# One-hots laid out by columns, past counts added in PSUM by VectorE, and a preparation handed to the first block's products: a convolution, router and mixture-of-experts kernel

## The chip, the cores and the metric

The kernel runs on one core of a Trainium2 chip. The metric is the device time of one execution in microseconds. The engines are called as in the profile: PE (TensorE, matrix products; PEld its weight loads), DVE (VectorE), ACT (ScalarE), POOL (GpSimd) and SP (SyncE, which issues most of the DMAs). SBUF is the working memory, PSUM the memory into which PE writes.

## The reference

```python
def _attn_ref(x, weight):                      # x [8, 3584, 192], weight [8 heads, 7 taps]
    w = softmax of weight over the taps
    x_pad = np.concatenate([zeros of 6 rows, x], axis=1)
    ...
    out = np.einsum('hk,bskhg->bshg', w, x_unf)   # each head's 24 columns: causal filter of 7 taps

def _moe_ref(x, w_skip, w_gate, w1, w2):       # x [28672, 192], 8 experts, w1 [8, 192, 1024], w2 [8, 1024, 192]
    do_compute = x @ w_skip > 0
    out = x.copy()
    xc = x[do_compute]
    logits = xc @ w_gate
    e_idx = np.argmax(logits, axis=1)
    ...                                        # probs: softmax of the logits
    gate_w = probs[np.arange(len(xc)), e_idx]
    for e in range(E):
        mask = e_idx == e
        h = np.maximum(xc[mask] @ w1[e], 0.0)
        y[mask] = gate_w[mask, None] * (h @ w2[e])
    out[do_compute] = xc + y
    return out
```

Tokens go through a causal filter; those with a positive skip score then go through the expert with the highest logit, weighted by its probability. All is fp32.

## The kernel before

**Phase 1** goes over the 8 batches. A batch of 3584 tokens is 30 columns (`NC`) of 120 tokens (`R`), with the token on the partition. `conv_heads` makes the filter as products with banded matrices, and ACT copies the results to `ys`, from where SP stores them to the output. Behind the heads of a batch, in small steps written out by hand (`IR`, `RR`, `PICK`), run the routing of the batch before (`route`: `router`, then `slots`) and the inversion of an earlier one (`invert`). The routines are generators: each `yield` hands over to the next, and the order in which the instructions are emitted is the order in which each engine runs them (`manual_schedule`).

**`slots`** finds each token's place in its expert's list. From the logits `lg` (9 for each token: 8 experts and the skip score) DVE makes the maximum (L546), the differences `df` (L550), the keys `kq` (L555), their minimum `km` (L560, L562) and from these the one-hots `oh`, fp16, 8 experts for each of 240 = 30 x 8 pairs (L566). PE then makes two products with `oh`: with a matrix of ones, for the count of each expert in each column (L571), and with a triangular matrix, for each token's rank in its column (L573). Between them a third product, fp32 with one row, adds `hist[b]`, the counts of all past batches, to the first column of each expert (L572). All three write the PSUM tile `pr`. DVE sums the counts over the columns with a scan (L583), adds the ranks (L589), copies the last column to `hist[b + 1]` (L591), takes the entry of the token's own expert by a product with `oh` (L598) and a sum (L601), and the slots are split for the inversion (L604 to L633).

**`invert`** turns slots into lists of token numbers: DVE makes one-hots `oa` and `ob` of the slot's row and column (L658), PE multiplies them and accumulates in `inv` (L646).

**The blocks.** 256 tokens of one expert make a block (128 for some). The first eight blocks (`TAIL`, `NTAIL`) come from the lists of the first five batches and are worked on while the last batches are routed. `gather` fetches the rows `y` (POOL, L829), `prep` scales and splits them to fp16 (DVE L845 to L362, ACT L853 and L854, DVE L859) and transposes them into `m` by DMA (SP, L862). `up` and `down` are the two products (L888, L939) with the Relu and the split of its result between them (ACT L909, DVE L911); `finish_rows` adds the result to the rows (L925), and POOL scatters it (L927). `weave` runs such a product's generator and at each of its steps a step of the routing and inversion that is left (`tail_slot`), and `n` pieces of the preparations in the list that it is given.

During the last batch's heads `step7` gathers four blocks and gives out pieces of the preparations of the first `PREP0` = 3 blocks, `PSEQ[h]` at head h. A call of `prep_piece` runs one `next` of the current preparation; one that has ended is dropped, and the call goes on with the next block.

```python
PSEQ = (0, 0, 4, 3, 4, 3, 4, 3)
TAIL = ("2221", "2221")
PREP0 = 3
```

The weights of the experts are split to two fp16 parts in the background (`split_weights`, ACT L327, DVE L338); what is left of it after the last head is emitted at once (`background(-1)`).

Of the kernel before, what the change touches and what calls it, by code (L numbers as in the profile page):

```python
# [8 lines left out]
F16 = mybir.dt.float16  # L9
I32 = mybir.dt.int32  # L10
AF = mybir.ActivationFunctionType
ALU = mybir.AluOpType
# [8 lines left out]
E, F = 8, 1024  # L21
NTOK = B * S
NF = F // P
R = 120
# [3 lines left out]
NC = -(-S // R)  # L28
# [43 lines left out]
FIRSTP = ((), ("", "y4"), ("", "y5"))  # L72
# [19 lines left out]
AHEAD = 5  # L92
PREP = 3
PREP0 = 3
MBUF = 4
PU = 2
# [6 lines left out]
def conv_router_moe(ctx: ExitStack, tc: tile.TileContext, x, weight, w_skip, w_gate, w1, w2, out):  # L103
    nc = tc.nc
# [11 lines left out]
    wk1 = ph1.enter_context(tc.tile_pool(name="wk1", bufs=2, side="right"))  # L116
# [47 lines left out]
    ones32 = const.tile([1, P], F32, name="ones32")  # L164
# [10 lines left out]
    ones16 = const.tile([P, P], F16, name="ones16")  # L175
# [77 lines left out]
    um1 = const.tile([P, P], F16, name="um1")  # L253
# [112 lines left out]
    hist = const.tile([P, B + 1, E], F32, name="hist")  # L366
# [168 lines left out]
    def slots(b, lg):  # L535
        def t3(name):
            return wk1.tile([R, NC, E], F32, tag=name, bufs=1, name=f"{name}{b}")

        def t2(name, dt=F32, bufs=1):
            return wk1.tile([R, NC], dt, tag=name, bufs=bufs, name=f"{name}{b}")  # L540

        def bc(t):
            return t.unsqueeze(2).broadcast_to([R, NC, E])
# [10 lines left out]
        kq = t3("kq")  # L554
        nc.vector.scalar_tensor_tensor(out=kq, in0=df, scalar=0.0,  # L555
                                       in1=pri[0:R].unsqueeze(1).broadcast_to([R, NC, E]),
                                       op0=ALU.is_equal, op1=ALU.mult)
        yield
        km = t2("km")
# [2 lines left out]
        nc.vector.scalar_tensor_tensor(out=km, in0=lg[:, 0:NC, E], scalar=0.0, in1=km,  # L562
                                       op0=ALU.is_le, op1=ALU.add)
        yield
        oh = wk1.tile([R, E, NC], F16, tag="oh", name=f"oh{b}")
        nc.vector.tensor_tensor(out=oh.rearrange("p e c -> p c e"), in0=kq, in1=bc(km), op=ALU.is_equal)  # L566
        yield HOP
        if in_tail:
            yield HOP
        pr = ps_ms.tile([P, 2, E, NC], F32, tag="ms", name=f"pr{b}")  # L570
        nc.tensor.matmul(pr[:, 0], ones16[0:R, :], oh, start=True, stop=False)  # L571
        nc.tensor.matmul(pr[:, 0, :, 0], ones32, hist[0:1, b, :], start=False, stop=True)  # L572
        nc.tensor.matmul(pr[0:R, 1], um1[0:R, 0:R], oh, start=True, stop=True)  # L573
        sm = t2("sm")
        nc.vector.tensor_reduce(out=sm, in_=ex, axis=AX.X, op=ALU.add)
        yield
# [2 lines left out]
        gt = gate_all[0:R, b, :]  # L579
        nc.vector.reciprocal(out=gt, in_=sm)  # L580
        yield HOP
        run = wk1.tile([P, E, NC], F32, tag="df", bufs=1, name=f"run{b}")
        nc.vector.tensor_tensor_scan(out=run.rearrange("p e c -> p (e c)"),  # L583
                                     data0=smask.rearrange("p e c -> p (e c)"),
# [3 lines left out]
        rs = wk1.tile([R, E, NC], F32, tag="kq", bufs=1, name=f"rs{b}")  # L588
# [4 lines left out]
        if b == REL:  # L593
# [1 line left out]
            yield  # L595
            nc.vector.scalar_tensor_tensor(out=hist[:, b + 1, 0:NA], in0=eoff[:, 0:NA], scalar=float(KH * P),
                                           in1=hist[:, b + 1, 0:NA], op0=ALU.add, op1=ALU.max)
        nc.vector.tensor_tensor(out=rs, in0=rs, in1=oh, op=ALU.mult)  # L598
        yield HOP
        sl = t2("sl")  # L600
        nc.vector.tensor_reduce(out=sl, in_=rs.rearrange("p e c -> p c e"), axis=AX.X, op=ALU.add)  # L601
# [11 lines left out]
                                op=ALU.is_ge)  # L613
# [177 lines left out]
    def early(what, after):  # L791

        if what:
            nc.gpsimd.tensor_copy(pace, after)
            gather(blocks[int(what[1])])

    preps, begun = [], [0]

    def prep_piece():
        if not preps:  # L800
            if begun[0] == PREP0:
                return
            preps.append(prep(blocks[begun[0]]))
            begun[0] += 1
        if next(preps[0], preps) is preps:
            preps.pop(0)
            prep_piece()
# [33 lines left out]
    def prep(k):  # L841

        am = k.am = wk2.tile([P, 2], F32, tag="yam", bufs=6, name=f"yam{k.n}")
        sc = wk2.tile([P, 2], F32, tag="ysc", bufs=3, name=f"ysc{k.n}")
        nc.vector.tensor_reduce(out=am[:, 0:k.us], in_=k.y[:, 0:k.us], axis=AX.X, op=ALU.max, apply_absolute_value=True)  # L845
        yield
        yield from pow2_steps(am[:, 0:k.us], sc[:, 0:k.us])
        yield


        yt = wk2.tile([P, 2, 4 * P], F16, tag="yt", bufs=3, name=f"yt{k.n}")
        for u in range(k.us):
            nc.scalar.activation(yt[:, u, 0:D], k.y[:, u, :], AF.Copy, scale=sc[:, u:u + 1])  # L853
            nc.scalar.activation(yt[:, u, 3 * P:], k.y[:, u, D - P:D], AF.Copy, scale=sc[:, u:u + 1])  # L854
        yield
        k.m = wk2.tile([P, 4, BLK], F16, tag="m", bufs=MBUF, name=f"m{k.n}")
        for u in range(k.us):
            for (a, b_, o) in ((P, D, D), (0, P, D + 64)):
                nc.vector.scalar_tensor_tensor(out=yt[:, u, o:o + b_ - a], in0=k.y[:, u, a:b_],  # L859
                                               scalar=sc[:, u:u + 1], in1=yt[:, u, a:b_],  # L860
                                               op0=ALU.mult, op1=ALU.subtract)
            nc.sync.dma_start_transpose(out=k.m[:, :, u * P:(u + 1) * P], in_=yt[:, u, :])  # L862
            yield
# [7 lines left out]
    def bank(pools):  # L871
        pools.append(pools.pop(0))
        return pools[-1]

    def up(k, wt):
        k.hh = wk3.tile([P, NF, BLK], F16, tag="hh", bufs=2, name=f"hh{k.n}")
        k.hl = wk3.tile([P, NF, BLK], F16, tag="hl", bufs=2, name=f"hl{k.n}")
        w = k.us * P
        fs = 2 * BLK // w
        split = len(ph_pools) > 1  # L880
        banks = []

        def open_bank(f0):
            banks.append(bank(ph_pools).tile([P, 2 * BLK], F32, tag="ph", name=f"ph{k.n}_{f0}")
                         .rearrange("p (f w) -> p f w", w=w))

        def product(ph, f, o, m, q, start, stop):
            nc.tensor.matmul(ph[:, f % fs, :], wt[q, o + f * P:o + (f + 1) * P], k.m[q, m, 0:w], start=start, stop=stop,  # L888
                             skip_group_check=split)

        if split:


            for f0 in range(0, NF, fs):
                open_bank(f0)
            for i in range(0, len(banks), 2):
                for j in range(fs):
                    for h in range(2):
                        product(banks[i + h], (i + h) * fs + j, OW1L + F, 1 + 2 * h, slice(64 * h, 64 * h + 64), j == 0, False)
        for f0 in range(0, NF, fs):  # L900
            if not split:
                open_bank(f0)
            ph = banks[f0 // fs]
            for f in range(f0, f0 + fs):
                seq = ((OW1, 0), (OW1, 2), (OW1 + F, 1), (OW1L, 0)) + (() if split else ((OW1L + F, 1),))
                for n, (o, m) in enumerate(seq):
                    product(ph, f, o, m, slice(0, P), n == 0 and not split, n == len(seq) - 1)
            hh = k.hh[:, f0:f0 + fs, 0:w]
            nc.scalar.activation(hh, ph, AF.Relu)  # L909
            yield  # L910
            nc.vector.scalar_tensor_tensor(out=k.hl[:, f0:f0 + fs, 0:w], in0=ph, scalar=0.0, in1=hh,  # L911
                                           op0=ALU.max, op1=ALU.subtract)
# [39 lines left out]
    blocks = []  # L952
# [42 lines left out]
    def weights_of(n):  # L995
        k = blocks[n]
        return wts[k.e] if k.l is None else dynw[k.l]
# [170 lines left out]
    def tail_slot():  # L1168

        background()  # L1170
        if not listed:
            turns((routes, 0), (routes, 1), (inversions, 0))
            if not routes and not inversions:
                finish(final_lists())
                listed.append(True)
        elif tables:
            if next(tables[0], tables) is tables:
                tables.pop()

    def weave(gen, preps=(), n=0, first=()):  # L1180

        k, *first = first or (None,)
        for f, _ in enumerate(gen):
            if first and f % 2 == 0:
                early(first.pop(0), k.hh[0:1, f * 2 * BLK // (k.us * P), 0:1])
            tail_slot()
            for _ in range(n):
                for p in list(preps):
                    if next(p, p) is p:
                        preps.remove(p)  # L1190
                    else:
                        break

    routes.append(whole_route(B - 1))
    in_tail.append(1)
    gathered, prepped = AHEAD - 1, PREP0
    ahead = []
    while preps or begun[0] < PREP0:
        prep_piece()
    bg.extend(save_weights(e, wts[e]) for e in range(NA))  # L1200
    weave(up(blocks[0], weights_of(0)), first=(blocks[0], *FIRSTP[0]))
    for n in range(NBLK):
        k = blocks[n]
        if 0 < n < 5:
# [30 lines left out]
        if n < 2:  # L1235
            gathered = AHEAD + n
# [15 lines left out]
    with tc.If(left > 0):  # L1252
# [9 lines left out]
        for c in range(B * NC):  # L1262
            nc.gpsimd.indirect_dma_start(
                out=list_dr, out_offset=bass.IndirectOffsetOnAxis(ap=slot[0:R, c:c + 1], axis=0),
                in_=ids[0:R, c:c + 1], in_offset=None, bounds_check=E * SPAN - 1, oob_is_err=False)
        for e in range(E):
            first = nc.values_load(lo_hi[0:1, e:e + 1], min_val=0, max_val=NTOK // BLK)
            last = nc.values_load(lo_hi[0:1, E + e:E + e + 1], min_val=0, max_val=NTOK // BLK)
            with tc.For_i(first, last, 1) as i:
# [4 lines left out]
                    out=k.si, in_=list_dr[bass.ds(i * BLK + e * SPAN, BLK), :].rearrange("(u p) o -> p (u o)", p=P))  # L1274
# [35 lines left out]
```

## Time and profile before

| | us |
|---|---|
| median of three runs | 684.56 (684.56 to 689.15) |
| the profiled execution | 686.43 |
| its span, first to last instruction | 684.7 |
| busy in the span: PE, DVE, ACT, POOL | 656.2, 544.3, 352.1, 271.0 |
| L566, one-hots, eight times | 9.7 |
| L571 + L572 + L573, products, matmuls alone | 2.1 + 3.3 + 2.6 |
| L598, product with the one-hots, eight times | 4.7 |

The profile is of one execution. A row of a group names line, engine, operation, output and inputs, their shapes and the count; behind the bar stand the busy time of the group, the mean of one in ns, and how long the engine idled just before, with what released it. A row with "min/median/max" is of the view of one line. Busy times of PE overlap, since its matmuls are pipelined; what one costs is better read from the distance between starts.

### The profile page before, as it was taken

To read this page: it belongs to the slowest core of one execution; us is meant where nothing else is said; L and a number is where in the kernel's file an instruction comes from. 1 tells how busy PE (TensorE), PEld (TensorE's weight loads), DVE (VectorE), ACT (ScalarE), POOL (GpSimd) and SP (SyncE) were. 2 spreads that over 40 slices of the span, in tenths; PEclk is the share of its full clock that TensorE was granted. 3 is DMA by queue.
4 is the path that set the end of the run, shared out by engine and by line. 5 is a ranking of instruction groups with operands and counts; after the bars stand their busy time and mean duration, and the time that the engine had idled before them with its cause. 6 is when DMAs were issued, how large, how long until landed. Compare 5 with 4: busy or idle time off the path is not lost.

```text
span 684.7 us, 17904 instructions
## 1 busy us (share of the span) xinstructions
PE 656.2 (96%) x6586; PEld 563.9 (82%) x6586; DVE 544.3 (79%) x1617; ACT 352.1 (51%) x762; POOL 271.0 (40%) x301
## 2 busy tenths in 40 slices
PE   8999998999697999989999999999999999999995
PEld 7667676766587898979999899999999899999995
DVE  8159999988989989886997897888888876666652
ACT  4776585558742334554464464564554644444421
POOL 4111111124113454644554554644544555554322
PEclk9999999999999999999999999999999999999999
DMA  7999999962941657466359369578567456999970
GB/s 214 322 322 313 300 286 326 326 217 66 246 145 47 161 143 153 89 181 182 82 170 216 89 175 193 105 175 177 126 181 157 132 148 175 272 291 330 326 211 15
DMA packets 169127, 133.31 MB, mean 195 GB/s; under 512 B 74320, under 2 KB 155986, under 8 KB 169028
## 3 DMA queue, kind: packets, MB, share of 16 engines
q1 hardware_dynamic: 157988, 110.26, 60.1%
q0 software_dynamic: 11040, 21.80, 11.8%
q8 instruction: 54, 0.88, 0.5%
q14 instruction: 45, 0.37, 0.2%
HBM read 69.70 MB, written 48.04 MB: 172 GB/s over the span
## 4 chain that ended last, share of the span: by engine, by line
PE 55%; DVE 0%; POOL 0%; POOLq 0%; issue 0%
PE ph L888 28%; PE po L939 27%; POOL out_dram L927 0%; DVE hl L911 0%; POOLq L1251 0%; DVE yt L859 0%; DVE o L925 0%
## 5 line engine op out<-in xcount | busy, mean ns | idle before, releaser
L909 ACT ACTIVATE hh<-ph 128x512 f16<-128x512 f32 x230 | 136.2, 593 | 227.1 <-PE ph L888 226.1
L888 PE MATMUL ph<-m,wt 128*128 128x256 f16 (+2 forms) x2000 | 210.0, 270 | 4.4 <-DVE hl L911 2.8
L888 PEld LDWEIGHTS <-wt 128*128 128x128 f16 (+1 forms) x2000 | 167.5, 98 | 38.7 <-issue 17.9
L939 PE MATMUL po<-wt,hh 128*128 128x192 f16 x1536 | 194.2, 246 | 0.0
L911 DVE SCALAR_TENSOR_TENSOR hl<-ph,hh 128x512 f16<-128x512 f32 x230 | 157.5, 686 | 40.9 <-ACT hh L909 40.5
L939 PE MATMUL po<-wt,hl 128*128 128x192 f16 x768 | 188.9, 246 | 0.0
L939 PEld LDWEIGHTS <-hh 128*128 128x128 f16 x1840 | 166.5, 98 | 1.1
L927 POOL DMA_INDIRECT out_dram<-o,sidx x82 | 85.8, 1046 | 138.7 <-DVE o L925 119.4
L829 POOL DMA_INDIRECT y<-out_dram,sidx x82 | 85.3, 1041 | 26.8 <-issue 10.1
L939 PEld LDWEIGHTS <-hl 128*128 128x128 f16 x920 | 90.0, 98 | 0.0
L393 PE MATMUL pc<-xs,toep 128*120 128x384 f32 (+1 forms) x224 | 77.3, 467 | 0.0
L925 DVE SCALAR_TENSOR_TENSOR o<-po,yf,y 128x192 f32<-128x192 f32 x115 | 47.2, 417 | 37.0 <-PE po L939 30.8
L859 DVE SCALAR_TENSOR_TENSOR yt<-y,ysc,yt 128x64 f16<-128x64 f32 x230 | 62.2, 313 | 14.8 <-ACT yt L853 13.2
L395 ACT COPY ys<-pc 120x768 f32<-120x768 f32 (+1 forms) x56 | 42.6, 761 | 40.7 <-PE pc L393 31.8
L853 ACT ACTIVATE yt<-y,ysc 128x192 f16<-128x192 f32 x115 | 51.4, 447 | 19.4 <-DVE ysc L362 13.8
L393 PEld LDWEIGHTS pc<-xs,toep 128*120 128x120 f32 x224 | 36.5, 183 | 14.1 <-issue 0.4
L854 ACT ACTIVATE yt<-y,ysc 128x128 f16<-128x128 f32 x115 | 44.8, 389 | 0.0
L338 DVE SCALAR_TENSOR_TENSOR wt<-raw,ar,wt 128x512 f16<-128x512 f32 x56 | 42.2, 759 | 1.4 <-ACT wt L327 1.4
L327 ACT ACTIVATE wt<-raw,ar 128x512 f16<-128x512 f32 x56 | 38.9, 724 | 5.3 <-DVE ar L362 5.3
L888 PE MATMUL ph<-m,wd 128*128 128x256 f16 (+3 forms) x440 | 40.6, 258 | 0.0
L939 PE MATMUL po<-wd,hh 128*128 128x192 f16 x304 | 38.4, 246 | 0.0
L888 PEld LDWEIGHTS <-wd 128*128 128x128 f16 (+1 forms) x440 | 32.9, 97 | 6.6 <-issue 3.4
(213 smaller groups left out, 778.8 us busy)
## 6 DMA issues: line engine op xcount, KB each, us to landing
wd<-wscr SPq DMA_DIRECT2D x44, 449.0 KB
wscr<-wt SPq DMA_DIRECT2D x84, 128.0 KB
xs<-in_x_dram SPq DMA_DIRECT2D x7, 1440.0 KB
xs<-in_x_dram SPq DMA_DIRECT2D x7, 1248.0 KB
out_dram<-ys SPq DMA_DIRECT2D x6, 1344.0 KB
out_dram<-ys SPq DMA_DIRECT2D x6, 1092.0 KB
raw<-in_moe_w_dram SPq DMA_DIRECT2D x32, 192.0 KB
raw<-in_moe_w_dram SPq DMA_DIRECT2D x8, 512.0 KB
```

The lines of the kernel that those rows point to most:

```text
L393: nc.tensor.matmul(pc[0:R, i, 0:n * G], toep[:, h + i, :], xs[b, half][:, :, (h + i) * G:(h + i + 1) * G], start=True, stop=True)
L395: nc.scalar.copy(ys[b, half][0:R, :, h * G:(h + 2) * G].rearrange("p g (h c) -> p h g c", c=G), pc[0:R, :, 0:n * G].rearrange("p i (g c) - ...
L829: rows_apart(nc.gpsimd.indirect_dma_start(out=k.y[:, u, :], out_offset=None, in_=out[0:k.rows, :], in_offset=bass.IndirectOffsetOnAxis(ap= ...
L853: nc.scalar.activation(yt[:, u, 0:D], k.y[:, u, :], AF.Copy, scale=sc[:, u:u + 1])
L854: nc.scalar.activation(yt[:, u, 3 * P:], k.y[:, u, D - P:D], AF.Copy, scale=sc[:, u:u + 1])
L859: nc.vector.scalar_tensor_tensor(out=yt[:, u, o:o + b_ - a], in0=k.y[:, u, a:b_], scalar=sc[:, u:u + 1], in1=yt[:, u, a:b_], op0=ALU.mult, ...
L888: nc.tensor.matmul(ph[:, f % fs, :], wt[q, o + f * P:o + (f + 1) * P], k.m[q, m, 0:w], start=start, stop=stop, skip_group_check=split)
L909: nc.scalar.activation(hh, ph, AF.Relu)
L911: nc.vector.scalar_tensor_tensor(out=k.hl[:, f0:f0 + fs, 0:w], in0=ph, scalar=0.0, in1=hh, op0=ALU.max, op1=ALU.subtract)
L925: nc.vector.scalar_tensor_tensor(out=o[:, u, :], in0=part, scalar=f2[:, u:u + 1], in1=k.y[:, u, :], op0=ALU.mult, op1=ALU.add)
L927: rows_apart(nc.gpsimd.indirect_dma_start(out=out[0:k.rows, :], out_offset=bass.IndirectOffsetOnAxis(ap=k.si[:, u:u + 1], axis=0), in_=o[: ...
L939: nc.tensor.matmul(part, lhs[:, f, u * P:(u + 1) * P], wt[:, w + f * D:w + (f + 1) * D], start=(n == 0), stop=(n == 3 * NF - 1))
```

## The change

Four edits. The one-hots are laid out with the expert innermost, so that L566 writes them in order; PE reads them in order as before and writes `pr`, whose layout stays, with a stride of one expert's 30 columns; L598 reads them with a stride of 8. The product with `hist` goes, and DVE adds `hist[:, b, :]` to the first column of each expert in PSUM, ahead of the scan. The loop that runs the remaining pieces of the preparations ahead of the first block's up products goes; the preparation at hand is given to the first block's `weave`, two pieces (`PU`) at a step; `prepped`, the number of preparations begun, is taken from the counter.

```diff
-        oh = wk1.tile([R, E, NC], F16, tag="oh", name=f"oh{b}")
-        nc.vector.tensor_tensor(out=oh.rearrange("p e c -> p c e"), in0=kq, in1=bc(km), op=ALU.is_equal)
+        oh = wk1.tile([R, NC, E], F16, tag="oh", name=f"oh{b}")
+        nc.vector.tensor_tensor(out=oh, in0=kq, in1=bc(km), op=ALU.is_equal)
...
-        nc.tensor.matmul(pr[:, 0], ones16[0:R, :], oh, start=True, stop=False)
-        nc.tensor.matmul(pr[:, 0, :, 0], ones32, hist[0:1, b, :], start=False, stop=True)
-        nc.tensor.matmul(pr[0:R, 1], um1[0:R, 0:R], oh, start=True, stop=True)
+        nc.tensor.matmul(pr[:, 0].rearrange("p e c -> p c e"), ones16[0:R, :], oh, start=True, stop=True)
+        nc.tensor.matmul(pr[0:R, 1].rearrange("p e c -> p c e"), um1[0:R, 0:R], oh, start=True, stop=True)
...
+        nc.vector.tensor_tensor(out=pr[:, 0, :, 0], in0=pr[:, 0, :, 0], in1=hist[:, b, :], op=ALU.add)
         run = wk1.tile([P, E, NC], F32, tag="df", bufs=1, name=f"run{b}")
...
-        nc.vector.tensor_tensor(out=rs, in0=rs, in1=oh, op=ALU.mult)
+        nc.vector.tensor_tensor(out=rs, in0=rs, in1=oh.rearrange("p c e -> p e c"), op=ALU.mult)
...
-    gathered, prepped = AHEAD - 1, PREP0
-    ahead = []
-    while preps or begun[0] < PREP0:
-        prep_piece()
+    gathered, prepped = AHEAD - 1, begun[0]
+    ahead = list(preps)
     bg.extend(save_weights(e, wts[e]) for e in range(NA))
-    weave(up(blocks[0], weights_of(0)), first=(blocks[0], *FIRSTP[0]))
+    weave(up(blocks[0], weights_of(0)), ahead, PU, first=(blocks[0], *FIRSTP[0]))
```

## The prediction

> **What bounds the kernel now.** I read the page's totals first, then the busy time by stretches, then the chain of work that ended last, and last who waited for whom.
>
> ```profile
> span 684.7 us, 17904 instructions
> PE 656.2 (96%) x6586; PEld 563.9 (82%) x6586; DVE 544.3 (79%) x1617; ACT 352.1 (51%) x762; POOL 271.0 (40%) x301
> ```
>
> PE is busy for 96% of the span, so what can be won without taking work from PE is at most 684.7 - 656.2 = 28.5 us. The next view tells where those lie: a stretch, its length, then busy time (and instructions) of PE, weight loads, DVE, ACT and POOL, the granted clock, the DMA share and GB/s. Two rows of the chain follow.
>
> ```profile
> 60.00:90.00 30.00, 30.00 (x222) 22.00 (x221) 28.77 (x87) 18.34 (x39) 3.49 (x6) 1.00 0.98 303
> 90.00:120.00 30.00, 28.05 (x215) 19.65 (x214) 27.91 (x86) 20.54 (x43) 3.11 (x6) 1.00 1.02 311
> 120.00:150.00 30.00, 28.66 (x230) 20.83 (x229) 27.58 (x80) 16.12 (x37) 3.14 (x5) 1.00 0.98 308
> 150.00:180.00 30.00, 25.29 (x195) 18.16 (x193) 26.91 (x95) 23.50 (x54) 13.11 (x18) 1.00 0.43 95
> 180.00:210.00 30.00, 26.24 (x259) 22.74 (x257) 26.27 (x81) 14.25 (x33) 3.81 (x5) 0.94 0.53 173
> 210.00:240.00 30.00, 25.84 (x285) 24.23 (x283) 29.19 (x97) 9.85 (x22) 11.43 (x12) 1.00 0.44 114
> ...
> 302.35 5.64 PE ph L888 x35
> 307.99 3.96 PE po L939 x48
> ```
>
> From 302 us on the chain is PE alone, up products and down products back to back; nothing of the change lies there, so what is won before 302 us moves the whole rest forward. Before that, PE is full until 90 us, idles 2.0 + 1.3 us from 90 to 150 us and 4.7 + 3.8 + 4.2 us from 150 to 240 us, with DVE busy for 26 to 29 of every 30 us. So phase 1 goes by PE as long as DVE keeps up, and its last third by DVE in good part. Which of PE's waits belong to lines that change?
>
> ```profile
> PE pr L571 <- DVE oh L566: 6.8, 4, 2.7
> PE inv L646 <- DVE ob L658: 4.4, 4, 2.2
> DVE inva L687 <- PE inv L646: 2.6, 1, 2.6
> PE pr L571 <- DVE oh L566: 2.0, 1, 2.0
> PE pr L571 <- DVE oh L566: 1.1, 1, 1.1
> PE pr L571 <- DVE oh L566: 3.8, 2, 2.7
> ```
>
> (Waiter and releaser; total us, times, longest. The first three rows are from the whole span, the last three from the stretches 90 to 120, 150 to 180 and 180 to 210 us.) The count product's wait for the one-hots holds PE for 6.8 us in four of the eight batches: 2.0, 1.1, 2.7 and 1.1. No row has PE waiting for `hist`.
>
> **The change part by part.**
>
> *One-hots by columns.*
>
> ```profile
> L566 DVE TENSOR_TENSOR oh<-kq,km 120x240 f16<-120x240 f32 x8 | 9.7, 1211 | 0.3
> L550 DVE TENSOR_TENSOR df<-lg,lm 120x240 f32<-120x240 f32 x8 | 3.2, 405 | 0.0
> L601 DVE TENSOR_REDUCE sl<-rs 120x30 f32<-120x240 f32 x8 | 4.7, 590 | 0.1
> L575 DVE TENSOR_REDUCE sm<-ex 120x30 f32<-120x240 f32 x8 | 3.2, 396 | 0.0
> L598 DVE TENSOR_TENSOR rs<-rs,oh x8: 403/408/1115, 46.6 to 213.0; 120x240 f32<-120x240 f32 x8
> ```
>
> L566 and L550 have the same engine, operation class, size and broadcast operand; L566 alone writes 2-byte elements 60 bytes apart, and it takes 1211 ns where L550 takes 405. Written in order it should cost L550's time: 0.81 us less, 8 times 6.5 us of DVE. In return L598 reads the one-hots 16 bytes apart. L601 reads 120 bytes apart and takes 590 where the same reduction in order, L575, takes 396: +0.19 us. I take that for L598 because it too is a read; the ends are 0 and the +0.81 of L566's write.
>
> *Counts added by DVE.*
>
> ```profile
> L605 DVE TENSOR_TENSOR bstart<-hist,eoff 128x8 f32<-128x8 f32 x8 | 1.3, 158 | 0.0
> L589 DVE SCALAR_TENSOR_TENSOR rs<-run,pr 120x240 f32<-120x240 f32 x8 | 3.2, 403 | 0.2
> ```
>
> The new addition has L605's size with an operand in PSUM, which costs L589 nothing beside L550. I take 0.17 us (0.16 to 0.25). It waits for both products, as the scan right behind it did already, so nothing new is queued behind a wait; the scan and the slots come 0.17 us later after it. DVE in a batch: -0.81 + 0.19 + 0.17 = -0.45 us, in all -3.6 us (-5.2 to +2.0).
>
> On PE the `hist` product goes, with its fp32 weight loads, and both one-hot products now write PSUM 120 bytes apart.
>
> ```profile
> L571 PE MATMUL pr<-oh,ones x1: 263/263/263, 109.4 to 109.4; 120*128 120x240 f16 x1
> L573 PE MATMUL pr<-oh,um x1: 313/313/313, 109.9 to 109.9; 120*120 120x240 f16 x1
> L888 PE MATMUL ph<-m,wt 128*128 128x256 f16 x1520 | 178.2, 274 | 1.5 <-DVE hl L911 1.1 <-ACT ys L395 0.4
> L888 PE MATMUL ph<-m,wt 128*128 128x128 f16 x152 | 9.3, 219 | 0.0
> L573 PEld LDWEIGHTS <-um 120*120 120x120 f16 x8 | 1.1, 135 | 0.2
> ```
>
> From L571 to L573 pass 0.5 us; without the product between them, the next one can start after its own weight load, 0.13 us: -0.37 us a batch (the first two rows are those of one batch, the others the means of the whole span). The price of the stride is shown by no row. A matmul costs (274 - 219) / 128 = 0.43 ns a column in order. The nearest row is L601, 4-byte elements apart: 590 - 396 = 194 ns over 240 elements, +0.81 ns on DVE's 1.04 ns ((405 - 158) / 232 gives 1.06). The same ratio of 1.8 on 0.43 ns is +0.08 us a product, +0.16 us a batch; I take that, so PE's net is -0.2 us a batch. The ends are 0 and the 0.81 us that L566 pays, 16 times 13 us.
>
> [...]
>
> *Third block's preparation.* The pieces given out by `PSEQ` are 4+3+4+3+4+3 = 21, and a block of two sub-blocks has 7 (one yield behind the maximum, two in the scales, one behind them, one behind ACT's copies, two with the transposes). So after the last head three blocks are through to their last yield, and the loop that goes only finds an ended generator. The trace agrees:
>
> ```profile
> 174.56 0.46 ACT L853 ACTIVATE yt<-y,ysc 128x192 f16<-128x192 f32 x1 [1.14 <-issue]
> ...
> 175.86 1.93 ACT L327 ACTIVATE wt<-raw,ar 128x512 f16<-128x512 f32 x3
> ...
> 177.69 0.57 ACT L909 ACTIVATE hh<-ph 128x512 f16<-128x512 f32 x1
> ```
>
> The third block's L853 stands on ACT ahead of the weight splits that are flushed after the last head. I count 0 for this edit: no instruction moves, nor any DMA on SP's or POOL's queue.
>
> *The sum.* To 150 us PE leads: 5 batches x 0.2 = 1.0 us. The 2.0 us wait shrinks by its own 0.81 and by what DVE won earlier (2 batches x 0.45 from 60 us on, less PE's 3 x 0.2): 1.1 us. For the `ob` waits I add 0.3 us. At the copy of `inva`, DVE waits for PE (2.6 us), so leads end there. From 150 to 220 us the waits of 1.1, 2.7 and 1.1 us shrink by 0.81 each, 2.4 us; the last stall there is
>
> ```profile
> 219.81 0.55 PE L646 MATMUL inv<-ob,oa 120*128 120x216 f16 x4 [2.16 <-DVE ob L658]
> ```
>
> and sees only DVE's net of 0.45 in the last batch, so 0.36 us go back: 2.1 us. Together 1.0 + 1.1 + 0.3 + 2.1 = **4.5 us**. The span would be 680.2 us. The profiled execution took 686.43 us with its span of 684.7; the median of the runs is 684.56, so I set the 4.5 us against the median: **680.0 us** (0.7% less). I do not count PE's saved products from 150 us on, where its next wait is for DVE.
>
> **The rivals.**
>
> *A. The forecast*, -2 to -6.8 us, 677.8 to 682.5: chance 0.55.
>
> *B. Most of it is taken back.* If L598 pays 0.81 us, DVE's net is +0.17 us a batch, the one-hots still come 0.81 us earlier, but the inversions later; then 1.0 us of PE's products, 0.8 us of the 2.0 us wait and 0.8 of the 2.7 us wait remain, 2.6 us at most. The other way to the same end is the DMA share of 0.98 to 1.02 from 60 to 150 us: if the next batch's rows became the bound, the 2.4 us won there would go. Against this: no row has PE waiting for `xs`. -2 to +1 us, 682.5 to 685.5: chance 0.19.
>
> *C. The clock gives more.*
>
> ```profile
> 182.00:184.00 2.00, 0.00 (x0) 0.00 (x0) 1.90 (x5) 2.00 (x5) 0.00 (x0) 1.00 0.91 328
> 184.00:186.00 2.00, 1.99 (x10) 1.77 (x10) 2.00 (x6) 0.88 (x2) 0.00 (x0) 0.55 0.99 381
> 186.00:188.00 2.00, 2.00 (x14) 1.70 (x14) 1.93 (x7) 1.75 (x3) 0.00 (x0) 0.60 0.99 361
> ...
> 304.00:306.00 2.00, 2.00 (x12) 1.35 (x10) 1.10 (x4) 0.99 (x2) 1.39 (x3) 0.50 0.77 115
> ```
>
> After the 2.7 us wait for the one-hots the clock is at 0.55 and 0.60 for 4 us, 0.45 x 2 + 0.40 x 2 = 1.7 us of PE lost; a like drop follows at 304 us. Waits shorter by 0.8 us or more can spare one or both: 4.5 + 1.7 to 4.5 + 3.4 us, and with DVE's net at its best end (5.2 in place of 3.6) up to 9.5: 675.0 to 677.7. Chance 0.19. [...]
>
> *D. Strided products cost more than the rest saves: slower.* Ahead of the stride the change is worth 4.5 + 16 x 0.08 = 5.8 us. At 0.36 us a product that is used up, at 0.79 it is slower by over 1%, and at L566's 0.81 us it is 5.8 - 13.0 = 7.2 us slower, 691.8. Against it: the output is 4-byte elements, as in L601, and not L566's 2-byte ones. Over 685.5 us: chance 0.07, of which 0.05 is slower by over 1%.
>
> **How the numbers follow.** The likeliest is A: 680.0. A range of 675.0 to 686.0 holds A, B, most of C and the near side of D, and leaves about 0.12 out; it covers DVE's net down to -5.2 us, and on the other side a stride of 0.45 us a product. One per cent, 6.85 us, is about what a measurement of this kernel can tell from no change. Faster by over 1% (under 677.7): C, 0.19, and a little of A, 0.20. Slower by over 1% (over 691.4): 0.05. The rest is within 1%: 0.75.
>
> **What would show it.** Right: L566 at 0.40 us; 16 fewer matmuls; a new DVE addition of about 0.17 us in eight; L598 near 0.59; the start of L573 at 0.15 to 0.25 us behind L571; the wait for the one-hots down from 6.8 to about 3 us; the unbroken chain of PE from about 298 us; ACT's order around 175 us unchanged. Wrong: L571 or L573 over 0.6 us long, or the next PE instruction behind them so late (D); L598 at 1.2 us (B); new waits of PE for `ys` or `m` in place of the one-hots; a clock of 1.00 from 184 to 188 us (C).

## The result, and the profile after

The changed kernel takes **680.02 us** (median of 10 runs, 679.39 to 682.17) against 684.97 us for the kernel before (median of 10, 683.08 to 689.15): ratio 0.9922, 95% interval 0.9903 to 0.9941. The forecast was 680.0 us. The profiled execution took 682.17 us, the longest of the ten. Executions more than 1.5% above the fastest of their kernel are left out of the ratios below, and the trace of `e3_hist_only`, which is of such a one, is read for its first 150 us alone.

The page's totals of the changed kernel, and its busy time by stretches (columns as in the prediction):

```profile
span 680.5 us, 17879 instructions
PE 655.4 (96%) x6570; PEld 562.8 (83%) x6570; DVE 540.9 (79%) x1625; ACT 351.7 (52%) x762; POOL 269.4 (40%) x301
```

```profile
90.00:120.00 30.00, 28.85 (x222) 20.50 (x221) 27.89 (x87) 21.34 (x47) 2.84 (x5) 1.00 1.03 315
120.00:150.00 30.00, 28.48 (x227) 20.66 (x226) 26.54 (x80) 15.45 (x36) 5.10 (x10) 1.00 0.96 303
150.00:180.00 30.00, 25.77 (x191) 18.37 (x190) 28.99 (x103) 24.17 (x55) 10.10 (x13) 0.95 0.51 128
180.00:210.00 30.00, 27.68 (x271) 23.58 (x271) 26.56 (x87) 13.54 (x31) 6.71 (x8) 0.94 0.44 147
210.00:240.00 30.00, 26.89 (x302) 25.56 (x300) 29.15 (x103) 10.85 (x25) 9.47 (x9) 1.00 0.48 124
```

There are 16 matmuls fewer (6586 before) and 8 instructions of DVE more (1617). PE's busy total hardly moves, 656.2 to 655.4 us; what went is its idle time between 90 and 240 us (16 us before, 12.3 now).

Last who waited for whom, over the whole span of the changed kernel (total us, times, longest):

```profile
PE inv L646 <- DVE ob L658: 4.9, 4, 2.3
...
PE pr L571 <- DVE oh L566: 2.5, 4, 1.2
```

The wait for the one-hots fell from 6.8 to 2.5 us (to 3.6 in the trace of `e5_changed`, a second measurement of the same kernel; why it differs is said with the late waits below); those for `ob` rose from 4.4 to 4.9. The lines that the diff touches, each in the view of its line (duration in ns, min/median/max; first and last start in us). L572 is now the rank product, which was L573:

```profile
L566 DVE TENSOR_TENSOR oh<-kq,km x8: 407/408/410, 43.3 to 201.0; 120x240 f16<-120x240 f32 x8
L571 PE MATMUL pr<-oh,ones x8: 362/366/560, 44.4 to 201.6; 120*128 120x240 f16 x8
L572 PE MATMUL pr<-oh,um x8: 407/408/688, 44.6 to 201.7; 120*120 120x240 f16 x8
L581 DVE TENSOR_TENSOR pr<-pr,hist x8: 161/166/174, 45.1 to 206.4; 128x8 f32<-128x8 f32 x8
L598 DVE TENSOR_TENSOR rs<-rs,oh x8: 578/596/614, 46.5 to 208.8; 120x240 f32<-120x240 f32 x8
```

Where did the lead arise? The list of the first five batches is copied by L687 and completed by L1050; these are marks of PE's and DVE's progress. Before, then changed (start in us), and the first row of the unbroken chain of PE, which began at 302.35 us:

```profile
L687 DVE COPY inva<-inv x1: 383/383/383, 151.0 to 151.0; 128x216 f32<-128x216 f32 x1
L1050 DVE TENSOR_TENSOR inva<-inva,inv x1: 369/369/369, 241.1 to 241.1; 128x216 f32<-128x216 f32 x1
```

```profile
L687 DVE COPY inva<-inv x1: 382/382/382, 149.2 to 149.2; 128x216 f32<-128x216 f32 x1
L1050 DVE TENSOR_TENSOR inva<-inva,inv x1: 372/372/372, 236.9 to 236.9; 128x216 f32<-128x216 f32 x1
```

```profile
298.32 5.64 PE ph L888 x35
```

The lead is 1.8 us at 150 us and 4.2 us at L1050; from there to the end of the span both take 443.6 us (684.7 - 241.1, 680.5 - 236.9). All of the difference between these two profiled executions is made before 241 us, where the prediction had put it.

### The profile page after: what moved, and what is told of

It reads as the page before. It is cut to its first block, busy times and chain, and to the rows that moved or that the text cites. A ratio compares the mean times of both kernels' runs of the same rounds, so it can differ in the third digit from the quotient of the medians.

```text
span 680.5 us, 17879 instructions
## 1 busy us (share of the span) xinstructions
PE 655.4 (96%) x6570; PEld 562.8 (83%) x6570; DVE 540.9 (79%) x1625; ACT 351.7 (52%) x762; POOL 269.4 (40%) x301
## 4 chain that ended last, share of the span: by engine, by line
PE 55%; DVE 0%; POOL 0%; POOLq 0%; issue 0%
PE ph L888 28%; PE po L939 27%; POOL out_dram L927 0%; DVE hl L911 0%; POOLq L1249 0%; DVE yt L859 0%; DVE o L925 0%
## 5 line engine op out<-in xcount | busy, mean ns | idle before, releaser
L306 DVE TENSOR_REDUCE am<-raw 128x1 f32<-128x512 f32 x56 | 38.0, 678 | 0.7 <-DMA raw<-in_moe_w_dram 0.4
```

## The experiments

All ratios are to the kernel before on the same chip, with 95% intervals. The experiments ran on three occasions, each on another chip. On the first (`e1` to `e4`) and third (`e9` to `e12`) the kernel before took 720.02 and 710.49 us and on the second (`e5` to `e8`) 684.7 us; so a time is compared only with others of its occasion. The first question is which edit brought the gain; the rival to "one-hots earlier and the product gone" was that the third edit or the clock did.

**The third edit alone** (`e1_prep_only`): before, with only this.

```diff
-    gathered, prepped = AHEAD - 1, PREP0
-    ahead = []
-    while preps or begun[0] < PREP0:
-        prep_piece()
+    gathered, prepped = AHEAD - 1, begun[0]
+    ahead = list(preps)
...
-    weave(up(blocks[0], weights_of(0)), first=(blocks[0], *FIRSTP[0]))
+    weave(up(blocks[0], weights_of(0)), ahead, PU, first=(blocks[0], *FIRSTP[0]))
```

> The kernel before with the third edit alone (the loop of remaining pieces gone, the preparation at hand given to the first block's products). Theory: that preparation is through to its last yield, so no instruction moves: 0 us, ratio 1.000 within noise, same order around 175 us. Rival: the edit carries part of the gain by taking work off DVE and ACT ahead of the first products: -1 to -2 us.

719.37 us, ratio 1.0007 (0.9964 to 1.0049). Up to 340 us each engine's instructions start in the same order as before; behind that three small memsets of DVE change places with a neighbour. The edit does nothing, since the third block's preparation has run to its end when the loop comes. In the changed kernel ACT's order is also that of before, 3.2 us earlier:

```profile
171.40 0.46 ACT L853 ACTIVATE yt<-y,ysc 128x192 f16<-128x192 f32 x1 [1.16 <-issue]
...
172.69 1.93 ACT L327 ACTIVATE wt<-raw,ar 128x512 f16<-128x512 f32 x3
174.53 0.58 ACT L909 ACTIVATE hh<-ph 128x512 f16<-128x512 f32 x1
```

**The one-hots alone** (`e2_onehot_only`, and the same kernel again as `e11_onehot_only`): before, with the new layout and the product with `hist` kept. The new lines, with the kept product among them:

```diff
+        oh = wk1.tile([R, NC, E], F16, tag="oh", name=f"oh{b}")
+        nc.vector.tensor_tensor(out=oh, in0=kq, in1=bc(km), op=ALU.is_equal)
...
+        nc.tensor.matmul(pr[:, 0].rearrange("p e c -> p c e"), ones16[0:R, :], oh, start=True, stop=False)
         nc.tensor.matmul(pr[:, 0, :, 0], ones32, hist[0:1, b, :], start=False, stop=True)
+        nc.tensor.matmul(pr[0:R, 1].rearrange("p e c -> p c e"), um1[0:R, 0:R], oh, start=True, stop=True)
...
+        nc.vector.tensor_tensor(out=rs, in0=rs, in1=oh.rearrange("p c e -> p e c"), op=ALU.mult)
```

> The kernel before with the one-hots by columns alone: the hist product stays on PE, both one-hot products write with a stride, L598 reads with a stride. Theory (the waits for the one-hots are the main term): the wait at 109 us nearly goes (-2.0), the late waits shrink by 2.2 and the inversions' by 0.3, PE pays 0.2 us a batch for the strides (+1.0): -3.5 us. Rival (the gain is PE's shorter work, waits only move elsewhere): 0 to +1 us, since PE has only more to do here.

> The kernel of e2 again. Theory, mended: PE pays 0.16 us a batch, the waits of batches 3 and 5 shrink by 0.81 each (-0.8 us together with the price at batch 5), and behind that DVE leads and gains its 0.62 and the 0.81 in batches 6 and 7: -2.5 to -3.2 us, 682; with e10 it adds up to the whole change. Rival: the two edits do not add up, and this one alone brings the whole 4 to 5 us.

714.9 us, 0.9953 (0.9916 to 0.9991), and 706.92 us, 0.995 (0.991 to 0.999).

**The counts alone** (`e3_hist_only`, again as `e10_hist_only`): before, with the addition by DVE in place of the product.

```diff
-        nc.tensor.matmul(pr[:, 0], ones16[0:R, :], oh, start=True, stop=False)
-        nc.tensor.matmul(pr[:, 0, :, 0], ones32, hist[0:1, b, :], start=False, stop=True)
+        nc.tensor.matmul(pr[:, 0], ones16[0:R, :], oh, start=True, stop=True)
...
+        nc.vector.tensor_tensor(out=pr[:, 0, :, 0], in0=pr[:, 0, :, 0], in1=hist[:, b, :], op=ALU.add)
```

> The kernel before with the counts added by DVE alone: one-hots and products in the old layout, no hist product. Theory: PE saves 0.37 us a batch but then waits longer for the one-hots at 109 us, and DVE has 0.17 us more a batch: 0 to -0.7 us. Rival (PE's shorter work carries the gain): 8 x 0.37, -3.0 us.

> The kernel of e3 again. Theory, mended: a wait of PE for the one-hots starts from PE's own logits, by way of ACT and DVE, so it moves with PE and does not grow; PE's 0.37 us a batch all show up to batch 5 (-1.9 us), and less behind it, where DVE leads with 0.17 us more a batch: -1.5 to -2.0 us, 683. Rival (what was expected of e3): 0 to -0.7 us. Rival (PE leads to the last batch): -3.0 us.

713.35 us, 0.9944 (0.9908 to 0.9981), and 707.62 us, 0.9933 (0.9897 to 0.9969). **My expectation for the first of these was wrong**: I took PE's saved products to be lost in a longer wait for the one-hots at 109 us. The wait stayed, and it came earlier. The count product of the fourth batch in `e3_hist_only`:

```profile
108.32 0.26 PE L571 MATMUL pr<-oh,ones 120*128 120x240 f16 x1 [1.94 <-DVE oh L566]
```

It starts at 108.3 us where it stood at 109.4, after a wait of 1.9 us (2.0 before). So the one-hots came earlier too. Why, the rows of DVE tell: its last idle time ahead of this wait and the first instruction of the batch's `slots`, before and then in `e10_hist_only`:

```profile
99.79 0.75 DVE L338 SCALAR_TENSOR_TENSOR wt<-raw,ar,wt 128x512 f16<-128x512 f32 x1 [0.52 <-ACT wt L327]
...
106.12 0.40 DVE L546 TENSOR_REDUCE lm<-lg 120x30 f32<-120x240 f32 x1
```

```profile
98.44 0.75 DVE L338 SCALAR_TENSOR_TENSOR wt<-raw,ar,wt 128x512 f16<-128x512 f32 x1 [0.37 <-ACT wt L327]
...
104.77 0.40 DVE L546 TENSOR_REDUCE lm<-lg 120x30 f32<-120x240 f32 x1
```

Both come 1.35 us earlier, and so does the product (109.37 and 108.01 us). DVE doesn't wait here for the logits, as I had expected for `e10_hist_only`: ACT had copied them by 102.8 us, and L546 starts at 106.12 without an idle time ahead of it. DVE's last wait is for ACT's split of a weight, and ACT itself last idled before that for a product of PE (`pl`, 0.44 us, until 94.92 us before and 93.58 us here). So the wait moves along with PE, by way of ACT's order of work, and a saving on PE ahead of it counts in full: 1.36 us by the fourth batch, about three times the 0.46 us found next.

What a batch of products costs PE is best read from the order of its instructions in the third batch, where it waits for nothing (start, length): before, then `e3_hist_only`, then `e2_onehot_only`, then changed.

```profile
85.88 0.27 PE L571 MATMUL pr<-oh,ones 120*128 120x240 f16 x1
...
86.54 0.55 PE L646 MATMUL inv<-ob,oa 120*128 120x216 f16 x4
```

```profile
85.29 0.27 PE L571 MATMUL pr<-oh,ones 120*128 120x240 f16 x1
85.39 0.27 PE L572 MATMUL pr<-oh,um 120*120 120x240 f16 x1
85.49 0.55 PE L646 MATMUL inv<-ob,oa 120*128 120x216 f16 x4
```

```profile
86.20 0.37 PE L571 MATMUL pr<-oh,ones 120*128 120x240 f16 x1
...
87.02 0.50 PE L646 MATMUL inv<-ob,oa 120*128 120x216 f16 x3
```

```profile
85.56 0.37 PE L571 MATMUL pr<-oh,ones 120*128 120x240 f16 x1
...
85.92 0.59 PE L646 MATMUL inv<-ob,oa 120*128 120x216 f16 x4
```

From L571 to the next line's product pass 0.66 us before, 0.20 without `hist`, 0.82 with the stride and `hist`, 0.36 in the changed kernel. The removed product is thus worth 0.46 us and the two strides cost 0.16 us, with and without it.

By their ratios the two halves bring 0.5% and about 0.6% and the whole 0.7 to 0.8%; the intervals of the halves are 0.7 to 0.8 points wide, so by time an overlap of the halves is likely and not shown. (The medians of the third occasion's executions are closer together still: 706.3 us for the counts and 706.7 for the one-hots, against 709.0 for the kernel before.) The traces show an overlap for the first 150 us. L687 starts at 151.0 us before, at 149.6 in both traces of the one-hots alone, at 149.0 and 148.7 in those of the counts alone, and at 149.2 and 149.0 in the changed kernel's: 1.4 us and 2.0 to 2.3 us alone, 1.8 to 2.0 together. Alone, the one-hots take away the wait for `ob` at 141 us, 1.3 us; with the counts it is back, at 1.5 us. Behind 150 us such a sum can't be drawn: L1050 starts at 240.8 and 238.7 us in the two traces of the one-hots alone.

**The changed kernel again** (`e5_changed`), beside the next three.

> The changed kernel itself, beside the three that follow. Theory (PE leads to the batch-5 products, each batch gives it 0.2 us, each wait for the one-hots on its path 0.81; behind that DVE leads and gives 0.45 + 0.81 a batch): the count products of batches 3, 5 and 6 start 1.4, 2.6 and 3.8 us earlier than in the kernel before where the clock is the same, the end 4.5 us. Rival (the one-hots' waits alone, 4 x 0.81): 0.8, 1.6, 2.4 and 3.2 us.

679.94 us, 0.9929 (0.9908 to 0.9950): the first result again. The count products of the fourth, sixth and seventh batch start at 107.78, 153.54 and 179.82 us, against 109.37, 156.26 and 184.01 before: 1.6, 2.7 and 4.2 us earlier, near the 1.4, 2.6 and 3.8 us of the theory and not the 0.8, 1.6 and 2.4 us of the rival. The last of them:

```profile
179.82 0.36 PE L571 MATMUL pr<-oh,ones 120*128 120x240 f16 x1 [1.88 <-DVE oh L566]
```

**The one-hots' write twice** (`e6_onehot_twice`): L566 issued a second time, 0.41 us more of DVE ahead of the products.

```diff
         nc.vector.tensor_tensor(out=oh, in0=kq, in1=bc(km), op=ALU.is_equal)
+        nc.vector.tensor_tensor(out=oh, in0=kq, in1=bc(km), op=ALU.is_equal)
```

> The changed kernel with the one-hots' instruction (L566) run twice, so that they come 0.41 us later and DVE has 0.41 us more a batch. Theory: the waits of PE for them grow by 0.41 each; the count products start later than in the changed kernel by 0 in the first three batches, 0.4 in batch 3, 0.8 in batch 5, 1.6 in batch 6 and 2.0 in batch 7; the end 2.0 us later. Rival (the waits are slack that the stretches behind them take up): batch 7 and the end as in the changed kernel.

681.9 us, 0.9966 (0.9949 to 0.9982), 2.0 us above the changed kernel, 1.4 at equal clock by the fit below. PE's waits from 90 to 120 us, of `e5_changed` and then of this kernel (L567 is the second write):

```profile
PE pr L571 <- DVE oh L566: 1.2, 1, 1.2
```

```profile
PE pr L572 <- DVE oh L567: 1.6, 1, 1.6
```

0.4 us more in the wait for 0.41 us more of DVE: each nanosecond of L566 goes straight into this wait. The 0.81 us that the new layout takes off it come out likewise, 2.0 to 1.2 us. Whether the end is later by as much is less sure. The times say 1.4 to 2.0 us. But in this kernel's trace the last batch's count product starts at 201.3 us and the addition of `inva` at 236.8, where `e5_changed` has 201.8 and 237.2, as the rival had it; the one trace of each had its slow stretch of the clock at another place (176 to 182 and 180 to 186 us).

**The products twice** (`e7_products_twice`): both strided products issued twice.

> The changed kernel with both strided products issued twice. Theory: PE has 0.2 us more for each strided product, 0.4 us a batch, and while it leads all of it shows: the count product of batch b starts 0.4 x b later up to batch 5 (+2.0), then DVE leads and little is added: the end +2 to +2.5 us. Rival A (a strided product is dear, up to 0.8 us): +8 us by batch 5. Rival B (phase 1 goes by DVE or by the DMA): +0 to +0.5.

681.29 us, 0.9944 (0.9927 to 0.9960), 1.35 us above changed, less than the 2 to 2.5 us expected. L571 (its first issue) of the sixth and of the last batch, in `e5_changed` and then here:

```profile
L571 PE MATMUL pr<-oh,ones x1: 362/362/362, 153.5 to 153.5; 120*128 120x240 f16 x1
...
L571 PE MATMUL pr<-oh,ones x1: 362/362/362, 201.8 to 201.8; 120*128 120x240 f16 x1
```

```profile
L571 PE MATMUL pr<-oh,ones x1: 363/363/363, 155.5 to 155.5; 120*128 120x240 f16 x1
...
L571 PE MATMUL pr<-oh,ones x1: 363/363/363, 202.6 to 202.6; 120*128 120x240 f16 x1
```

The delay is 2.0 us in the sixth batch, after five batches of products, and 0.8 us in the last. PE's products count in full as long as PE leads, and are in part absorbed afterwards. How large that part is stays rough: the addition of `inva` starts 1.5 us later (238.7 against 237.2), and the clock fell at other places here (176 to 184 and 216 to 222 us).

**Ranks by columns** (`e4_columns`, again as `e9_columns`): changed, but the rank product writes PSUM in order and `rs` has the expert innermost; of DVE's passes over the 240 elements behind the scan only the addition (L589) still reads an operand with a stride. The new lines, not all of them:

```diff
+        nc.tensor.matmul(pr[0:R, 1].rearrange("p e c -> p (e c)"), um1[0:R, 0:R], oh.rearrange("p c e -> p (c e)"), start=True, stop=True)
...
+        rs = wk1.tile([R, NC, E], F32, tag="kq", bufs=1, name=f"rs{b}")
...
+        nc.vector.tensor_tensor(out=rs, in0=rs, in1=oh, op=ALU.mult)
+        nc.vector.tensor_reduce(out=sl, in_=rs, axis=AX.X, op=ALU.add)
```

> The changed kernel with all behind the scan by columns: the rank product (L572) writes PSUM in order, the ranks' addition (L589) reads the scan's result with a stride and writes by columns, and L598 and L601 read in order. Theory: L572 0.41 to 0.31 us, L589 +0.19, L598 -0.19, L601 -0.19, so DVE -0.19 and PE -0.05 to -0.1 us a batch: 0.5 to 1.0 us below the changed kernel, 5.5 to 6 us below the kernel before. Rival (DVE behind the one-hots is off the path): no further gain.

> The kernel of e4 again (count product with the strided write, all behind the scan by columns), now to be set beside the changed kernel's time. Theory: the rank product's 0.1 us and DVE's 0.19 us a batch are won: count product of batch 3 at about 107.4 us, of batch 5 0.5 us ahead of the changed kernel's, the end 0.7 to 1.0 us below it, some 679.0. Rival: nothing behind the one-hots is on the path and the rank product's gain is lost in a wait: 680.0.

710.34 us, 0.9898 (0.9839 to 0.9956), and 706.33 us, 0.9928 (0.9893 to 0.9962). In the second's trace one strided DVE pass is left of two (L589 604 ns; the product and the sum, L599 and L602 there, 407 and 395 ns by their medians). Up to the fifth count product its two traces agree, 128.45 and 128.43 us, ahead of the changed kernel's 129.10 and 128.89 by about the 0.1 us a batch that the rank product was to save. At the addition of `inva` they no longer agree:

```profile
L1051 DVE TENSOR_TENSOR inva<-inva,inv x1: 368/368/368, 239.1 to 239.1; 128x216 f32<-128x216 f32 x1
```

That is `e4_columns`, in which the clock had fallen to 0.50 at 140 us; `e9_columns` has 235.8 us, and the changed kernel 236.9 and 237.2. So by the marks it is about 0.5 us ahead at the fifth batch, and neither these nor the times, which don't differ from the changed kernel's beyond the intervals, show that it beats it.

**The stride on the read** (`e8_columns_read`): like the last, but the count product too writes in order, and reads its one-hots 16 bytes apart instead.

```diff
+        nc.tensor.matmul(pr[:, 0], ones16[0:R, :], oh.rearrange("p c e -> p e c"), start=True, stop=True)
```

> All behind the scan by columns (rank product in order, L589 reading the scan with a stride, L598 and L602 in order), and the count product reads the one-hots with a stride of 16 bytes in place of writing PSUM with one. Theory: if only the strided write of PSUM is dear, L571 goes from 0.37 to 0.26 us and PE's net is -0.37 us a batch, as with the hist product gone alone: 1.0 us below the changed kernel at batch 5, 1 to 1.5 us below it at the end. Rival: the strided read costs the product as much (0.37 us), and only DVE's -0.19 a batch and the rank product's 0.1 are left, 0.5 us.

679.24 us, 0.9923 (0.9898 to 0.9947), which is no different from the changed kernel. The product itself was expected at 0.26 us, or by the rival at 0.37, and both were wrong:

```profile
L571 PE MATMUL pr<-oh,ones x8: 586/587/592, 44.4 to 201.2; 120*128 120x240 f16 x8
```

587 ns, against 366 with the strided write and 263 in order. On PE the strided read is the dearer of the two by 0.22 us.

**Idle products in the wait** (`e12_warm`): changed, with 24 idle products on PE ahead of the count product of the seventh batch, so that PE does not stand still in that wait.

```diff
+        if b == B - 2:
+            for _ in range(24):
+                nc.tensor.matmul(pr[:, 1].rearrange("p e c -> p (e c)")[:, 0:P], ones16, ones16, start=True, stop=True)
```

> The changed kernel with 24 idle matmuls (ones by ones, overwritten by the next product) ahead of batch 6's count product, 1.35 us of PE in a wait of 1.9 us. Theory (PE's idle time of 2.6 and 1.9 us behind each other is what lets the clock fall to half for some 4 us): the clock stays at 1.00 from 180 to 186 us and the end comes 0.8 to 1.7 us earlier. Rival: the drop comes whatever fills this wait; 0 us.

706.89 us, 0.9971 (0.9919 to 1.0023): inconclusive by time. The clock (the third number from the right) shows why. The changed kernel's first trace, then `e5_changed`, then `e12_warm`, then PE's order in the last:

```profile
176.00:178.00 2.00, 2.00 (x16) 1.63 (x15) 1.97 (x6) 0.00 (x1) 0.00 (x0) 0.71 0.55 126
```

```profile
176.00:178.00 2.00, 1.94 (x19) 1.66 (x18) 1.97 (x7) 0.00 (x0) 0.00 (x0) 1.00 0.54 129
...
182.00:184.00 2.00, 2.00 (x12) 1.60 (x11) 1.93 (x7) 1.76 (x3) 0.00 (x0) 0.50 1.00 359
```

```profile
176.00:178.00 2.00, 2.00 (x12) 1.69 (x12) 1.97 (x7) 0.00 (x0) 0.00 (x0) 0.50 0.56 127
```

```profile
175.39 1.52 PE L476 MATMUL tp<-ident,ys 120*128 120x120 f32 x8 [2.58 <-ACT ya L477]
...
179.40 1.50 PE L573 MATMUL pr<-ones 128*128 128x128 f16 x24
```

The clock is at 0.50 from 176 to 178 us, behind a wait of 2.58 us for `ya` and ahead of the idle products. So the drop does not need the wait for the one-hots, which it comes ahead of here. Its place differs even between two traces of one kernel: it is 176 to 184 us in the changed kernel's first trace and 180 to 186 us in `e5_changed` (184 to 188 us before). One trace of `e12_warm` therefore can't tell what the idle products did, and what decides the place stays open.

## Why the prediction was right, point by point

**The total** came out as forecast: 4.5 us, measured 4.95 us by the medians of the first measurement and 4.76 us in the second.

**PE's products, 1.0 us.** Right in kind and short in size: the stride costs 0.16 us a batch, as forecast from DVE's ratio, and the removed product 0.46 where I had 0.37, because without it the rank product starts 0.10 us behind the count product in `e3_hist_only`, less than its own weight load of 0.13 us: the load runs under that product (in the changed kernel's third batch from 85.56 to 85.69 us, the count product from 85.56 to 85.93). Net -0.30 us a batch in place of -0.20, 1.5 us in five batches.

The strided output does slow the matmul, L571 takes 366 ns where it took 263, and that gives the factor: (366 - 263) / 240 = 0.43 ns a column on the 0.43 ns worked out for one in order, so twice the time a column. On a product of 240 columns that is 0.1 us, or by the starts 0.16 us for both, against 0.46 us for the removed product; rival D's crossing stood at 0.36 us a product. (That crossing charges all 16 products in full, where the sum counts those of five batches alone; by the sum's own rule it is 5.3 / 10 = 0.53 us.)

**The wait of 2.0 us, 1.1 us.** It shrank by 0.8 us, its own L566 and no more. The step that failed is the further 0.3 us for "what DVE won earlier": DVE brings no lead of its own into this wait, because it idles for ACT ahead of it, 0.83 us until 96.3 and 0.51 us until 99.2 us in the changed kernel, 0.84 and 0.52 before. What it won in the earlier batches ends there, and the wait moves along with PE (`e3_hist_only`, `e10_hist_only`).

**The `ob` waits, 0.3 us.** Wrong: the one at 141 us grew (1.3 to 1.5 us from 120 to 150 us; all of them 4.4 to 4.9). PE had gained 0.2 us more up to there than DVE. In `e2_onehot_only`, where DVE gains and PE does not, no wait is left from 120 to 150 us.

These three give 1.5 + 0.8 - 0.2 = 2.1 us by 150 us where the forecast had 2.4; L687 shows 1.8, and 2.0 in `e5_changed` (149.0 us).

**The late waits, 2.1 us.** From L687 to L1050 pass 90.1 us before, 87.7 us in the changed kernel and 88.2 us in `e5_changed` (237.2 - 149.0): 2.4 and 1.9 us less. The waits for the one-hots from 150 to 210 us fell from 4.9 to 2.5 us in `e5_changed`: 1.10 to 0.32, 2.68 to 1.88 and 1.08 to 0.29, each by the 0.8 us of the forecast. Part of it went, as forecast, into other waits for DVE. In the first trace they fell to 1.4 us, but not by more gain: there the clock is at 0.50 from 178 to 182 us and PE reaches the second of these waits later, so the wait is 0.77 in place of 1.88 us, while the product starts at 180.06 in place of 179.82 us. The statement that PE's products do not count after 150 us is right in part: doubled, they cost 2.0 us at the sixth batch and 0.8 at the last.

**DVE.** Forecast 3.6 us less, measured 544.3 - 540.9 = 3.4 us. L566 fell to 408 ns (forecast 405), L598 rose by 0.19 us in the median, L581 takes 0.166 us (0.17). That the total fits so well is in part luck: L598's eight together rose by 0.1 us and not by 1.5, and L591's by 0.8 (2.1 to 2.9 us): their stalls moved, as told below.

**The third edit, 0.** Right by its own experiment.

**The rivals.** B's price, 0.81 us for L598, was not paid. D is answered above. C came true in a small part: the drop was not spared, and no run shows that a shorter wait spares one (with the wait for the one-hots down to 0.77 us, the changed kernel's first trace has the clock at 0.50 to 0.58 from 178 to 184 us); but the changed kernel's mean clock is a little higher, 0.9945 against 0.9926 over the executions of the second measurement. A line fitted through the times of that occasion against each execution's mean granted clock, with one level for each kernel, falls by 4.2 us per 0.01 of clock (standard error 0.5). At a clock of 0.995 it has the kernel before at 683.8 us and the changed one at 680.0 (0.2 and 0.4): 3.8 of the 4.8 us come at equal clock, and about 1 us with the clock. That is a fit, and no experiment held the clock fixed; the lead at L1050, 4.2 us and in `e5_changed` 3.9, agrees with it. So the forecast's 4.5 us is nearer to the median than its terms deserve, and that is luck: the products brought 0.5 us more than their term, the 2.0 us wait 0.3 less and the `ob` waits 0.5 less, which nearly cancels, and about 1 us came with the clock, which the sum did not count.

## What to carry to other kernels

When an operand's layout must be strided somewhere, put the stride where it is cheapest and off the critical wait: here, for the same 240 elements (rows' medians, strided and in order), a strided 2-byte write by DVE cost 0.8 us (L566, 1213 and 408 ns, 60 bytes apart), a 2-byte read by PE 0.3 (L571, 587 and 263 ns, 16 bytes), a 2-byte read by DVE 0.2 (L598, 596 and 408 ns, 16 bytes) and a 4-byte write by PE 0.1 (L571, 366 and 263 ns, 120 bytes). Before counting a saving as lost in the next wait, follow the awaited engine back to its own last idle time and on to what ended that; if the chain starts from the engine that was made faster, the wait moves along and the saving stays, as the 1.36 us by the fourth batch of `e10_hist_only` did. Before comparing a mark of two traces, look for a drop of the clock ahead of it; two traces of one kernel, `e4_columns` and `e9_columns`, lay 3.3 us apart behind one (0.50 at 140 us in the first). Read what a small matmul costs from the distance of the starts around it, with and without it: its own row and its weight load's gave 0.37 us where 0.46 was saved.

## What the runs showed of the hardware that I had not expected

**The strided read cost PE more than the strided write.** In `e8_columns_read` 2-byte elements 16 bytes apart take (587 - 263) / 240 = 1.35 ns a column more, three times the 0.43 of the changed kernel's write, 4-byte elements 120 bytes apart. No run shows what makes the difference, nor what another distance would cost.

**Two of DVE's instructions end only behind a copy of POOL.** L598's 590 ns of before were a mean of six runs near 0.41 us and two of 1.1 us. In the fourth batch DVE's copy and product, and POOL's copy, before and then changed:

```profile
112.82 0.17 DVE L591 COPY hist<-run 128x8 f32<-128x8 f32 x1
112.94 1.11 DVE L598 TENSOR_TENSOR rs<-rs,oh 120x240 f32<-120x240 f32 x1
```

```profile
112.86 0.94 POOL L455 COPY yc<-ys 120x896 f32<-120x896 f32 x1 [9.52 <-ACT ys L395]
```

```profile
111.42 0.40 DVE L589 SCALAR_TENSOR_TENSOR rs<-run,pr 120x240 f32<-120x240 f32 x1
111.74 0.44 DVE L591 COPY hist<-run 128x8 f32<-128x8 f32 x1
112.10 0.58 DVE L598 TENSOR_TENSOR rs<-rs,oh 120x240 f32<-120x240 f32 x1
```

```profile
111.22 0.94 POOL L455 COPY yc<-ys 120x896 f32<-120x896 f32 x1 [8.47 <-ACT ys L395]
```

Whichever of the two meets POOL's copy ends only behind it, L598 at 114.05 us behind 113.80 and L591 at 112.18 behind 112.16, so in the second and fourth batch the stall, 0.7 us on L598 before, now falls on L591 (0.73 and 0.44 us in place of 0.17), and the group of L598 costs hardly more than before, 4.8 us against 4.7. In the fifth batch it stood on L591 before as well (0.93 and 0.92 us). In the changed kernel's fourth batch L589 runs wholly under POOL's copy and takes 0.40 us there, as elsewhere. That POOL's copy is the cause was not tried by taking it away, and no run shows why L589 is spared.

**The same kernel takes another time on another chip.** On the first and third occasions the kernel before took 4 to 5% longer. There PE's second products of the blocks waited where nothing that the profile shows released them; this row is of `e1_prep_only`, from 240 to 660 us, and no such row stands in the traces of the second occasion:

```profile
PE po L939 <- issue: 9.6, 23, 1.0
```

What makes the difference stays open. Phase 1 ran alike where the clock did: `e1_prep_only`, in which it is that of the kernel before, has the fourth count product at 109.38 us against 109.37, and then, after the clock fell to 0.50 at 110 us, the fifth at 132.36 against 130.74. So times were not compared across occasions, and a mark behind such a drop is to be read with care.
